# An attention and two mixtures of experts in one kernel: TensorE's work of a period regrouped by block size, and zero fills moved ahead of the weight stream

## The chip, the cores and the metric

One Trainium2 chip, one core. The time is that of the device in microseconds, the median of the runs of one program; lower is better. A second figure, the span, is taken from one profiled execution and runs from its first to its last instruction.

## The reference

Attention over 4 batches and 8 heads of 576 positions of 64 numbers: a band (each position sees those less than 4 away) plus a downsampled part (queries, keys and values averaged by 4, the result repeated 4 times). Its output, 2304 rows of 512, goes through a soft mixture (8 experts of 4 slots), and that result through a second mixture that routes each row to its best 2 of 8 experts. Everything is float32.

```python
q_d = q.reshape(B, H, Sd, factor, D).mean(axis=3)      # k_d, v_d alike, factor 4
out_up = np.repeat(sm_attn(q_d, k_d, v_d), factor, axis=2)
mask = np.abs(pos[:, None] - pos[None, :]) < factor
scores = np.where(mask, scale * q @ k.T, -1e9)
x = softmax(scores) @ v + out_up                       # then (B*S, H*D)
logits = x @ phi                                       # 2304 x 32 slots
slot_input = softmax(logits, axis=0).T @ x             # per expert 4 x 512
slot_out[e] = relu(slot_input[e] @ w1[e]) @ w2[e]
x = softmax(logits, axis=1) @ slot_out
noisy = x @ w_gate + log1p(exp(x @ w_noise)) * noise   # best two experts per row
out[rows of e] += weight * (relu(x @ w1[e]) @ w2[e])
```

## The kernel before

**Attention in 16 units.** A unit is one batch and two heads. The units are pipelined by hand: one period of the loop works on four of them, in the order of the string `SEQ` (L19), whose words are the steps in the table `BL` (L550). The words that matter here, with the line of their work: `S` the band's scores (mask L285, products L289) and `SD` the downsampled scores (L300), of unit p; of unit p-1 `CP` (L375) and `CD` (L386), which turn the band's and the downsampled weights, `VD` (L268, L272), which averages the values, `DP` (L414) and `DD` (L421), which multiply weights by values; of unit p-2 `EP` (L441, L443), which turns the finished rows back, and `LG` (L463, L465), the logits of the soft mixture; of unit p+1 `A0` and `A1` (L231), which turn keys and queries, and `ld` (L186), which loads them for p+2; `lV` (L207) loads values. Copies out of PSUM are `cp` (L219 on ScalarE, L221 on VectorE): `EP00` to `EP11` into `PT`, `ED0` and `ED1` into `PdT`, `X0` and `X1` into `xK`, `V0` and `V1` into `Vd`, `x0` and `x1` into `xT`; `XA` (L433) adds the downsampled part, `LA` (L472, L474) adds up the logits. Every engine runs its own steps in the order in which they are written; one engine waits for another by semaphores where data or a buffer asks for it. The four buffers named `t` (`tp`, L176) take turns for all that TensorE turns; `S`, `Sd` and `xl` have a bank or two of PSUM of their own. In three of the periods each of the steps `ST`, `SU`, `SU_`, `SE`, `SS` (softmax over rows, kept up from batch to batch, L479 to L528) and `SK` (L534) are added.

**The tail** (`TSEQ`, L21) ends the last three units and the slots' input. `R2` there puts the loads of weights 8 to 10 (`w8` to `w10`) on SyncE's queue.

**Soft mixture.** Eight experts; each has a first product `hp` (L795), a turn of the hidden values `ht` (`hidden_t`, L807), and a second product `yacc` (L817). The weights come by DMA in the order of use; SyncE issues all loads (L101), and from the fourth expert's on they wait for buffers that `hidden(0)` frees.

**Routing and second mixture.** Rows are scattered into a table `tab` in DRAM and gathered by expert; the products (L1054) hold most of the second half. `tab` and `out` have to be zero before: 27 pieces in the list `fills`, the first 7 of them `tab`'s (six of 256 KB, one of 64 KB), sent by `clear` (L109) from a tile of zeros after the last weights of the soft mixture.

**Blocks.** TensorE's array of 128 by 128 is used in blocks: 128 by 128, 128 by 64, 128 by 32, 64 by 64, 16 rows by 64. In the trace a row for TensorE names the block (`128*64`).

Of the kernel before, what the change touches and what calls it, by code (L numbers as in the profile page):

```python
# [17 lines left out]

SEQ = """S SK CP EP01 ld EP10 M EP00 ST SD CD z EP11 ED0 EL SS MD A0 ED1 EX a00 W a01 SU SU_ A1 P1 a100 a101  # L19
a110 a111 P0 KD DQ0 VD z DP V0 V1 DQ1 DX EP LG DD x1 LA lV x0 X1 SE RD DM X0 XA""".split()  # L20
TSEQ = """S:15 CP:14 W EP01:14 EP00:14 SD:15 M:15 EL:15 EP10:14 EX:15 EP11:14 CD:14 ED0:14 MD:15 SU:15 VD:14 DP:14 V0:14 V1:14 EP:13  # L21
# [11 lines left out]
NHOT = [4, 8]  # L33
N2 = 3


@with_exitstack
def attn_moe_moe_kernel(ctx: ExitStack, tc: tile.TileContext, q, k, v, moe_phi, moe_w1, moe_w2,
# [50 lines left out]

    phi4 = const.tile([128, 4, 4 * NS], F32, name="phi4")  # L90
    wgn = const.tile([128, 4, 2 * E], F32, name="wgn")
# [14 lines left out]
    LK = keep.tile([128, NTILE, NS], F32, name="LK")  # L106
    zero = keep.tile([128, 256], F32, name="zero")

    def clear():  # L109
        o = fills.pop(0)  # L110
        n = o.shape[0]
        return nc.sync.dma_start(out=o.rearrange("p (a c) -> p a c", a=2), in_=zero[0:n, None].to_broadcast([n, 2, 256]))


    with ExitStack() as tctx:
# [33 lines left out]
        PT = a2.tile([128, 5, 2, 128], F32, name="PT")  # L149
        P = a2.tile([128, NG, 64], F32, name="P")  # L150
        Vs = [(a1, a2)[i].tile([128, 5, 2, D], F32, name=f"V{i}") for i in range(2)]
        four = a2.tile([128, 9, 32], F32, name="four")
# [23 lines left out]
        def tp():  # L176
            return ps.tile([128, 512], F32, name="t", bufs=4)

        LD, VQ, KD, DQ, SD, SS, PD, PL, XL, XT, XK = ({} for _ in range(11))

# [80 lines left out]
        def v_pe(u):  # L261

            V = Vs[u % 2]
            XL[u] = ps.tile([128, 2, 512], F32, name="xl")
            t = XL[u][:, 0, 290:418]
            for d in range(2):
                for c in range(4):
                    nc.tensor.matmul(t[32 * c:32 * c + 32], four[:, 5 * d + c],  # L268
                                     V[:, c + d].rearrange("p h d -> p (h d)"), start=(d == 0), stop=(d == 1),
                                     skip_group_check=True)  # L270
            for h in range(2):
                nc.tensor.matmul(XL[u][0:32, h, 434:498], four[:, 4], V[:, 4, h], start=True, stop=True,  # L272
                                 skip_group_check=True)
            VQ[u] = (None, wk.tile([128, 2, 128], F32, name="Vd", bufs=1))

        def v_evac(u, i):
            xl, Vd = XL[u], VQ[u][1]
            if i:
                cp("v1", Vd[0:16, 1].rearrange("p (h d) -> p h d", h=2), xl[0:16, :, 434:498])
            else:  # L280
                cp("v0", Vd[:, 0], xl[:, 0, 290:418])

        def b_s(u):
            s = ps.tile([128, 512], F32, name="S")
            nc.tensor.matmul(s[:, 0:NG * KW], idb, mask.rearrange("p g k -> p (g k)"), start=True, stop=True)  # L285
            for g in range(NG):
                for a in range(2):
                    c0 = 58 * g + HQ * a
                    nc.tensor.matmul(s[64 * a:64 * a + 64, KW * g:KW * g + KW],  # L289
                                     Q[:, c0:c0 + 32].rearrange("p i h -> p (i h)"), K[:, c0:c0 + KW],  # L290
                                     start=False, stop=True, skip_group_check=True)
            SS[u] = s

# [86 lines left out]
        def c_d(u):  # L380
            Ed = PD.pop(u)
            tt = []
            for kb in range(2):
# [4 lines left out]
                tt.append(t)  # L388
            PdT = wk.tile([128, 2, 2, 144], F32, name="PdT", bufs=1)
            CT[u, 1] = (PdT, tt)  # L390

# [7 lines left out]
        def c_ed(u, kb):  # L399
            PdT, tt = CT[u, 1]  # L400
            n = (128, 16)[kb]
            cp(f"d{kb}", PdT[0:n, kb].rearrange("p h (a i) -> p h a i", a=3),
               tt[kb][0:n, 0:288].rearrange("p (a h i) -> p h a i", a=3, h=2))
# [13 lines left out]
        def d_d(u):  # L417
            xl, PdT, Vd = XL[u], CT[u, 1][0], VQ.pop(u)[1]
            for kb, n in enumerate((128, 16)):
                for h in range(2):  # L420
                    nc.tensor.matmul(xl[64 * h:64 * h + 64, 1, 290:434], Vd[0:n, kb, 64 * h:64 * h + 64], PdT[0:n, kb, h],  # L421
                                     start=(kb == 0), stop=(kb == 1), skip_group_check=True)
# [14 lines left out]
        def e_pe(u):  # L437
# [6 lines left out]
            ET_[u] = (t, t2)  # L444
            if u % 4 == 0:
                XK[u // 4] = xp.tile([128, 5, 4, 128], F32, name="xK", bufs=1)

        def e_evac(u, i):
            t = ET_[u][i]
            if i:  # L450
# [7 lines left out]

        def logit_pe(u, t2=None):
            xT, kk = XT[u], u % 4  # L460
            L = (ET_[u][1] if t2 is None else t2)[:, 128:320]
            for t in range(4):
                nc.tensor.matmul(L[32 * t:32 * t + 32, 0:128], phi4[:, kk, 0:NS], xT[:, 128 * t:128 * t + 128],  # L463
                                 start=True, stop=True, skip_group_check=True)
            nc.tensor.matmul(L[:, 128:192], phi4[:, kk], xT[:, 512:576], start=True, stop=True, skip_group_check=True)  # L465
            LL[u] = L

# [118 lines left out]
        for p in range(-1, NU - 1):  # L586
            if p == 0:
                nc.sync.dma_start(out=phi4[:, :, 0:NS], in_=moe_phi.rearrange("(k p) s -> p k s", p=128))
            if p >= 5 and small:
# [5 lines left out]
            for nm in SEQ:  # L595
# [8 lines left out]
                if p == -1 and nm == "lV":  # L604
                    nc.gpsimd.memset(PT, 0.0)
                if p == -1 and nm == "DQ1":
                    nc.vector.memset(P, 0.0)
            if p == 0:
                hot(NHOT[0])
                nc.vector.tensor_scalar(trib, jp, 0.0, None, op0=ALU.is_gt)  # L610
                consts()
            if p == 1:
                nc.vector.tensor_copy(phi4[:, :, NS:4 * NS].rearrange("p k (t s) -> p k t s", t=3),
                                      phi4[:, :, None, 0:NS].to_broadcast([128, 4, 3, NS]))
        m = ms_[(B - 1) % 2]
# [8 lines left out]
        def ring_2():  # L624
            actx.close()
            ring2 = rctx.enter_context(tc.tile_pool(name="ring2", bufs=1, reuse_waits="tile"))
            for i in range(NPRE, NPRE + N2):
                mload(i, ring2, (f"w{i}a", f"w{i}b"))
            flush()

        def max_t():
# [30 lines left out]
        def slot_in():  # L662
            t = tp()
            for kk in range(4):
# [5 lines left out]
              "SI": slot_in, "UA": lambda: slot_u(B - 1, (0, 1)), "UB": lambda: slot_u(B - 1, (2, 3)),  # L670
              "LG:15": lambda: logit_pe(NU - 1, tp()), "W": flush}
        TAIL.append(1)
# [42 lines left out]
    with ExitStack() as mctx:  # L715
# [85 lines left out]
        def hidden_t(e):  # L801
            hs_ = HS.pop(e)
            hz[e] = mw.tile([128, 2, 4, NS], F32, name="hz", bufs=3)
            nc.gpsimd.memset(hz[e], 0.0)
            ht_ = ps.tile([128, 2, 4, NS], F32, name="ht", bufs=1)
            for c in range(2):
                nc.tensor.transpose(ht_[:, c].rearrange("p j s -> p (j s)"), hs_[:, 128 * c:128 * c + 128], idf)  # L807
            nc.vector.tensor_scalar(hz[e][:, :, :, SPE * e:SPE * e + SPE], ht_[:, :, :, SPE * e:SPE * e + SPE],
                                    0.0, None, op0=ALU.max)

# [592 lines left out]
```

## Time and profile before

| | us |
|---|---|
| median of 3 runs | 496.57 (494.85 to 496.62) |
| the profiled execution's own time | 494.55 |
| its span | 492.7 |
| TensorE busy, matmuls | 470.2 (95% of the span) |
| VectorE, ScalarE, GpSimd busy | 277.4, 263.4, 199.2 |
| mean granted clock of TensorE | 0.987 |

How to read it: PE is TensorE, PEld its weight loads, DVE VectorE, ACT ScalarE, POOL GpSimd, SP SyncE, and SPq the queue of SyncE, where DMA issues show. L and a number is the line in the kernel. A bracket at a row's end tells how long the engine stood before it and for whom; "issue" is standing that nothing in the profile explains. Attention runs to about 150 us, its tail and the slots' input to 164 us, the soft mixture to about 200 us, the rest to 492.7 us.

### The profile page before, as it was taken

To read this page: it belongs to the slowest core of one execution; us is meant where nothing else is said; L and a number is where in the kernel's file an instruction comes from. 1 tells how busy PE (TensorE), PEld (TensorE's weight loads), DVE (VectorE), ACT (ScalarE), POOL (GpSimd) and SP (SyncE) were. 2 spreads that over 40 slices of the span, in tenths; PEclk is the share of its full clock that TensorE was granted. 3 is DMA by queue.
4 is the path that set the end of the run, shared out by engine and by line. 5 is a ranking of instruction groups with operands and counts; after the bars stand their busy time and mean duration, and the time that the engine had idled before them with its cause. 6 is when DMAs were issued, how large, how long until landed. Compare 5 with 4: busy or idle time off the path is not lost.

```text
span 492.7 us, 12033 instructions
## 1 busy us (share of the span) xinstructions
PE 470.2 (95%) x4569; PEld 355.9 (72%) x4569; DVE 277.4 (56%) x720; ACT 263.4 (53%) x698; POOL 199.2 (40%) x289
## 2 busy tenths in 40 slices
PE   5999999899998999899999999999999999999993
PEld 4688877777875543467787787887887887878882
DVE  7878877777875321696579545273462544624300
ACT  2567766666775021486365465483664746727410
POOL 5565636536540100166566677422222221222222
PEclk9999999999999799999999999999999999999997
DMA  9999998989979599999988744699958856333333
GB/s 160 278 243 214 233 221 192 242 216 202 265 239 345 171 393 399 389 346 338 365 258 228 224 75 76 150 363 297 275 72 229 216 128 154 43 45 43 45 43 46
DMA packets 108423, 104.16 MB, mean 211 GB/s; under 512 B 68170, under 2 KB 78090, under 8 KB 108362
## 3 DMA queue, kind: packets, MB, share of 16 engines
q1 hardware_dynamic: 101450, 90.50, 61.2%
q0 software_dynamic: 6912, 12.85, 16.6%
q8 instruction: 38, 0.62, 0.5%
q14 instruction: 23, 0.19, 0.1%
HBM read 83.60 MB, written 19.73 MB: 210 GB/s over the span
## 4 chain that ended last, share of the span: by engine, by line
PE 73%; issue 9%; DMA 7%; DVE 3%; POOL 2%; ACT 2%; POOLq 2%; SPq 0%; ACTq 0%; DVEq 0%
PE y L1054 34%; DMA wr<-in_moe_w_dram 5%; PE S L289 4%; PE t L231 3%; PE gx L871 3%; PE xl L421 3%; PE Sd L300 3%; PE xl L414 2%; PE t L375 2%; PE xl L268 2%; PE t L441 2%; PE h L1034 2%; PE t L386 2%; POOL out_dram L1073 2%; POOLq L1079 1%
## 5 line engine op out<-in xcount | busy, mean ns | idle before, releaser
L1054 PE MATMUL y<-whi,hl 128*128 128x512 f32 x320 | 127.3, 398 | 0.0
L1054 PE MATMUL y<-whi,hh 128*128 128x512 f32 x320 | 126.7, 396 | 0.4 <-ACT hh L1035 0.4
L1054 PE MATMUL y<-wlo,hh 128*128 128x512 f32 x320 | 126.5, 395 | 0.0
L1073 POOL DMA_INDIRECT out_dram<-ys,idx x40 | 64.5, 1612 | 107.9 <-ACT ys L1065 56.3
L1065 ACT ACTIVATE ys<-y,gt 128x512 f32<-128x512 f32 x40 | 27.4, 686 | 82.4 <-issue 46.9
L1026 DVE TENSOR_TENSOR wlo<-wr,whi 128x512 fp32r<-128x512 f32 x64 | 42.0, 692 | 50.3 <-ACT whi L1023 49.9
L1054 PEld LDWEIGHTS y<-wlo,hh 128*128 128x128 f32 x320 | 60.1, 188 | 12.9 <-issue 1.0
L1054 PEld LDWEIGHTS y<-whi,hl 128*128 128x128 f32 x320 | 60.1, 188 | 12.3 <-issue 2.1
L1054 PEld LDWEIGHTS y<-whi,hh 128*128 128x128 f32 x320 | 60.2, 188 | 11.8 <-ACT hh L1035 0.6
L333 POOL TENSOR_TENSOR P<-El,su 64x350 f32<-64x350 f32 x31 | 23.9, 772 | 59.7 <-DVE su L326 38.3
L1036 DVE SCALAR_TENSOR_TENSOR hl<-h,hh 128x256 fp32r<-128x256 f32 (+1 forms) x64 | 31.3, 489 | 16.0 <-ACT hh L1035 14.7
L1000 POOL DMA_INDIRECT tab<-stk,pos x36 | 35.6, 990 | 11.5 <-issue 10.7
L1036 DVE SCALAR_TENSOR_TENSOR hl<-gx,hh 128x256 fp32r<-128x256 f32 (+1 forms) x64 | 31.2, 487 | 10.7 <-ACT hh L1035 9.1
L1023 ACT ACTIVATE whi<-wr 128x512 fp32r<-128x512 f32 x64 | 36.9, 625 | 0.2
L1035 ACT ACTIVATE hh<-gx 128x256 fp32r<-128x256 f32 (+1 forms) x64 | 28.1, 439 | 15.0 <-PE gx L1034 12.5
L1035 ACT ACTIVATE hh<-h 128x256 fp32r<-128x256 f32 (+1 forms) x64 | 28.0, 437 | 12.5 <-PE h L1034 10.2
L1072 POOL MEMSET spacer<- 1x1 f32 x40 | 13.6, 340 | 41.6 <-issue 41.6
L219 ACT ACTIVATE PT<-t 64x256 f32<-64x256 f32 (+1 forms) x50 | 20.6, 417 | 13.5 <-PE t L375 12.7
L919 DVE TENSOR_TENSOR oh<-iot,R 128x256 fp32r<-128x256 f32 (+2 forms) x50 | 20.3, 439 | 11.4 <-PE xs L937 9.6
L231 PE MATMUL t<-idf,ld 96*128 96x96 f32 x192 | 21.1, 259 | 4.9 <-DMA ld<-in_k_dram 4.3
L219 ACT ACTIVATE xT<-xl 128x290 f32<-128x290 f32 x32 | 11.5, 411 | 26.2 <-PE xl L421 24.1
L289 PE MATMUL S<-K,Q 128*64 128x35 f32 x640 | 23.1, 231 | 2.2 <-issue 1.4
(301 smaller groups left out, 837.8 us busy)
## 6 DMA issues: line engine op xcount, KB each, us to landing
wr<-in_moe_w_dram SPq DMA_DIRECT2D x120, 256.0 KB, 5.6
wr<-in_moe_w_dram SPq DMA_DIRECT2D x56, 512.0 KB, 7.1
out_dram<-zero SPq DMA_DIRECT2D x20, 256.0 KB, 3.4
V<-in_v_dram SPq DMA_DIRECT2D x62, 80.0 KB, 5.2
ld<-in_k_dram SPq DMA_DIRECT2D x32, 144.0 KB, 4.7
ld<-in_q_dram SPq DMA_DIRECT2D x32, 144.0 KB, 4.4
XT<-tab SPq DMA_DIRECT2D x5, 320.0 KB, 5.6
tab<-zero SPq DMA_DIRECT2D x6, 256.0 KB, 4.8
```

The source lines that it names most:

```text
L219: nc.scalar.activation(dst, src, AF.Copy)
L231: nc.tensor.transpose(t[:, 96 * c:96 * c + 96], ld[:, i, 3 * j + c].rearrange("p h d -> p (h d)"), idf[0:96, 0:96])
L289: nc.tensor.matmul(s[64 * a:64 * a + 64, KW * g:KW * g + KW], Q[:, c0:c0 + 32].rearrange("p i h -> p (i h)"), K[:, c0:c0 + KW], start=Fals ...
L333: eng.tensor_tensor(P[as_, :, HQ * a:HQ * a + KW], El[as_], su[as_, :, None].to_broadcast([64, NG, KW]), op=ALU.mult)
L1000: st = nc.gpsimd.indirect_dma_start(out=tab, out_offset=bass.IndirectOffsetOnAxis(ap=pos[:, c, i:i + 1], axis=0), in_=stk[:, i].bitcast(F3 ...
L1023: nc.scalar.activation(whi[:, kk], wb(kk), AF.Copy)
L1026: eng.tensor_tensor(wlo[:, kk], wb(kk), whi[:, kk].bitcast(F32), op=ALU.subtract)
L1035: nc.scalar.activation(hh[:, f], h, AF.Relu)
L1036: nc.vector.scalar_tensor_tensor(hl[:, f], h, 0.0, hh[:, f].bitcast(F32), op0=ALU.max, op1=ALU.subtract)
L1054: nc.tensor.matmul(y, l[:, kk, ts_], r_[:, kk], start=(m == 0), stop=(m == 23))
L1065: nc.scalar.activation(ys, YS.pop((e, ti)), AF.Copy, scale=gt[:, ti:ti + 1])
L1073: st = nc.gpsimd.indirect_dma_start(out=out, out_offset=bass.IndirectOffsetOnAxis(ap=idx[:, ti:ti + 1], axis=0), in_=ys, in_offset=None, c ...
```

## The change

Seven edits.

1. In `SEQ`, `EP` stands behind `CP` (ahead of `SD`), `LG` behind `VD`, `DD` behind `DP`, ahead of the next period's mask; `X0` and `X1`, the copies of `EP`, stand behind `EP11`; `LA` behind `V1`; `SU_` behind `SD`.
2. The mask product is made in two blocks of 128 by 64 instead of one of 128 by 128.
3. The logits' last 64 columns are made in four products of 32 columns instead of one of 128, so `phi` is held once and not four times; the product goes to the bank of `S` in the loop.
4. `DD`'s second block has 128 rows, of which 112 are zeros set once, instead of 16 rows; `Vd` and `PdT` are fixed buffers.
5. `hidden_t` makes eight products of 32 columns that pick the expert's own 4 slots, instead of two full turns.
6. Seven zero pieces (`NZ`) are issued right behind the loads of `w8` to `w10`.
7. The tile of zeros is 512 wide, and a packet of it 2 KB instead of 1 KB.

```diff
-SEQ = """S SK CP EP01 ld EP10 M EP00 ST SD CD z EP11 ED0 EL SS MD A0 ED1 EX a00 W a01 SU SU_ A1 P1 a100 a101
-a110 a111 P0 KD DQ0 VD z DP V0 V1 DQ1 DX EP LG DD x1 LA lV x0 X1 SE RD DM X0 XA""".split()
+SEQ = """S SK CP EP01 ld EP10 M EP00 ST EP SD SU_ EP11 X0 X1 CD z ED0 EL SS MD A0 ED1 EX a00 W a01 SU A1 P1 a100 a101
+a110 a111 P0 KD DQ0 VD LG z DP V0 V1 LA DQ1 DX DD x0 x1 lV SE RD DM XA""".split()
...
+NZ = 7
...
-    zero = keep.tile([128, 256], F32, name="zero")
+    zero = keep.tile([128, 512], F32, name="zero")
...
-        return nc.sync.dma_start(out=o.rearrange("p (a c) -> p a c", a=2), in_=zero[0:n, None].to_broadcast([n, 2, 256]))
+        return nc.sync.dma_start(out=o, in_=zero[0:n])
...
-            nc.tensor.matmul(s[:, 0:NG * KW], idb, mask.rearrange("p g k -> p (g k)"), start=True, stop=True)
+            for a in range(2):
+                as_ = slice(64 * a, 64 * a + 64)
+                nc.tensor.matmul(s[as_, 0:NG * KW], idb[:, as_], mask.rearrange("p g k -> p (g k)"), start=True, stop=True,
+                                 skip_group_check=True)
...
-            for kb, n in enumerate((128, 16)):
+            for kb in range(2):
                 for h in range(2):
-                    nc.tensor.matmul(xl[64 * h:64 * h + 64, 1, 290:434], Vd[0:n, kb, 64 * h:64 * h + 64], PdT[0:n, kb, h],
+                    nc.tensor.matmul(xl[64 * h:64 * h + 64, 1, 290:434], Vd[:, kb, 64 * h:64 * h + 64], PdT[:, kb, h],
                                      start=(kb == 0), stop=(kb == 1), skip_group_check=True)
...
-            L = (ET_[u][1] if t2 is None else t2)[:, 128:320]
+            L = (tp() if TAIL else SB[u + 2])[:, 0:192]
...
-            nc.tensor.matmul(L[:, 128:192], phi4[:, kk], xT[:, 512:576], start=True, stop=True, skip_group_check=True)
+            for t in range(4):
+                nc.tensor.matmul(L[32 * t:32 * t + 32, 128:192], phi[:, kk], xT[:, 512:576], start=True, stop=True,
+                                 skip_group_check=True)
...
+                    nc.gpsimd.memset(Vd[:, 1], 0.0)
+                    nc.gpsimd.memset(PdT[:, 1], 0.0)
...
             flush()
+            for _ in range(NZ):
+                clear()
...
-                nc.tensor.transpose(ht_[:, c].rearrange("p j s -> p (j s)"), hs_[:, 128 * c:128 * c + 128], idf)
...
+                for j in range(4):
+                    nc.tensor.matmul(ht_[32 * j:32 * j + 32, c], hs_[:, 128 * c + 32 * j:128 * c + 32 * j + 32], own_,
+                                     start=True, stop=True, skip_group_check=True)
```

What it moves on TensorE in one period of the loop: first before (from `VD` to the next period's `CD`; lines 268 and 272 are `VD`, 414 `DP`, 421 `DD`, 285 and 289 mask and `S`), then after, where the same steps have lines 271 and 275, 418, 425, 289 and 294, and `EP` is 445 and 447, `LG` 467 and 470.

```order
L268 MATMUL xl<-V_133,four 32x128 x8
L272 MATMUL xl<-V_133,four 32x64 x2
L414 MATMUL xl<-PT,V_133 64x58 x20
L441 MATMUL t<-idf,xT 128x128 x4
L443 MATMUL t<-idf,xT 64x128
L463 MATMUL t<-xT,phi_79 32x128 x4
L465 MATMUL t<-xT,phi_79 128x64
L421 MATMUL xl<-PdT,Vd 64x144 x4
L285 LDWEIGHTS idb
L285 MATMUL S<-mask,idb 128x350
L289 MATMUL S<-K,Q 64x35 x20
L375 MATMUL t<-idf,P 128x128 x5
```

The same stretch of the period after:

```order
L271 MATMUL xl<-V_135,four 32x128 x8
L275 MATMUL xl<-V_135,four 32x64 x2
L467 MATMUL S<-xT,phi 32x128 x4
L470 MATMUL S<-xT,phi 32x64 x4
L418 MATMUL xl<-PT,V_135 64x58 x20
L425 MATMUL xl<-PdT,Vd 64x144 x4
L289 LDWEIGHTS idb
L289 MATMUL S<-mask,idb 64x350
...
L294 MATMUL S<-K,Q 64x35 x20
L380 MATMUL t<-idf,P 128x128 x5
```

Between `DP` and `DD` there stood `EP` and `LG`, ten products; now `DD` follows `DP` at once, and `LG` stands ahead of `DP`. The pair of rows of the mask comes twice (the second is left out).

On ScalarE in one period, before and then after, from the copies of `x0` and `x1` (`xT`) to those of the queries (`Q`); a period's row of `El` is the exponential of the band's scores.

```order
L219 ACTIVATE xT<-xl 128x5x58 x2
L219 ACTIVATE xK<-t 64x128
L219 ACTIVATE xK<-t 128x4x128
L219 ACTIVATE PT<-t 64x3x128
L219 ACTIVATE PT<-t 64x2x128 x2
L219 ACTIVATE PdT<-t 128x288
L219 ACTIVATE PdT<-t 16x288
L319 ACTIVATE El<-El 128x350
L219 ACTIVATE K<-t 128x288 x2
L219 ACTIVATE Q<-t 64x288 x2
```

ScalarE's period after:

```order
L222 ACTIVATE xT<-xl 128x5x58 x2
L222 ACTIVATE PT<-t 64x3x128
L222 ACTIVATE PT<-t 64x2x128 x2
L222 ACTIVATE xK<-t 128x4x128
L222 ACTIVATE xK<-t 64x128
L222 ACTIVATE PdT<-t 128x288
L222 ACTIVATE PdT<-t 16x288
L324 ACTIVATE El<-El 128x350
L222 ACTIVATE K<-t 128x288 x2
L222 ACTIVATE Q<-t 64x288 x2
```

The two copies into `xK` stood ahead of those into `PT`; now they stand behind them and ahead of `PdT`, `El`, `K` and `Q`.

On SyncE at the end of attention, before and then after: the loads of the weights 9 and 10, and what follows them.

```order
L101 DMA w9b<-in_moe_w_dram 128x512 x4
L101 DMA w10a<-in_moe_w_dram 128x1024 x2
L101 DMA w10b<-in_moe_w_dram 128x1024 x2
L101 DMA wr<-in_moe_w_dram 128x512 x8
L101 DMA wr<-in_moe_w_dram 128x1024 x4
```

SyncE's queue there after:

```order
L102 DMA w9b<-in_moe_w_dram 128x512 x4
L102 DMA w10a<-in_moe_w_dram 128x1024 x2
L102 DMA w10b<-in_moe_w_dram 128x1024 x2
L113 DMA tab<-zero 128x512 x6
L113 DMA tab<-zero 32x512
L102 DMA wr<-in_moe_w_dram 128x512 x8
L102 DMA wr<-in_moe_w_dram 128x1024 x4
```

The seven pieces of `tab` now stand between the last early weights and the stream `wr`; the 20 pieces of `out` stay where they were.

## Rows read from the trace of the kernel before

**Rows 1.** The page's part 4: the chain that ended last, by line.
```profile
PE y L1054 34%; DMA wr<-in_moe_w_dram 5%; PE S L289 4%; PE t L231 3%; PE gx L871 3%; PE xl L421 3%; PE Sd L300 3%; PE xl L414 2%; PE t L375 2%; PE xl L268 2%; PE t L441 2%; PE h L1034 2%; PE t L386 2%; POOL out_dram L1073 2%; POOLq L1079 1%
```
**Rows 2.** Windows, one period: stretch, its length, busy us by engine, clock, DMA share, GB/s.
```profile
114.28:122.68 8.40, 8.40 (x155) 6.84 (x154) 6.51 (x18) 5.92 (x20) 4.83 (x8) 1.00 1.08 231
```
**Rows 3.** Timeline of that period's start: start us, us, engine line, operation, idle before.
```profile
111.34 0.81 PE L414 MATMUL xl<-PT,V 64*64 64x58 f32 x40
111.51 0.83 DVE L221 COPY Q<-t 64x288 f32<-64x288 f32 x2
112.38 0.48 DVE L221 COPY Vd<-xl 128x128 f32<-128x128 f32 x2
112.77 0.16 PEld L463 LDWEIGHTS t<-xT,phi 128*32 128x32 f32 x8 [0.20 <-issue]
113.13 0.30 PEld L465 LDWEIGHTS t<-xT,phi 128*128 128x128 f32 x2 [0.20 <-issue]
113.89 0.19 PEld L421 LDWEIGHTS xl<-PdT,Vd 16*64 16x64 f32 x4 [0.20 <-issue]
114.28 0.10 PEld L285 LDWEIGHTS <-idb 128*128 128x128 bf16 x1 [0.20 <-issue]
114.54 1.25 PEld L289 LDWEIGHTS S<-K,Q 128*64 128x64 f32 x40 [0.16 <-issue]
```
**Rows 4.** Chain of waits, same period and the next: start us, us, what.
```profile
112.15 0.59 PE t L441 x4
...
112.85 0.36 PE t L463 x8
...
115.90 0.70 PE t L375 x5
```
**Rows 5.** Chain of waits in the tail, unit 15's products.
```profile
150.75 0.78 PE xl L414 x40
...
151.56 0.49 DVE Vd L221 x2
...
152.18 0.88 PE xl L421 x8
```
**Rows 6.** Timeline, ScalarE in the periods around 108 to 115 us.
```profile
108.08 1.29 ACT L219 ACTIVATE PT<-t 64x384 f32<-64x384 f32 x3 [1.16 <-PE t L375]
...
109.39 0.69 ACT L219 ACTIVATE PdT<-t 128x288 f32<-128x288 f32 x2
...
115.00 0.75 ACT L219 ACTIVATE xK<-t 64x128 f32<-64x128 f32 x2
```
**Rows 7.** Timeline, VectorE in a period with slots.
```profile
63.99 0.64 DVE L528 COPY U<-t 128x512 f32<-128x512 f32 x1
```
**Rows 8.** Timeline, SyncE's queue: unit 15's queries are issued (two loads).
```profile
127.85 2.02 SPq L186 DMA_DIRECT2D ld<-in_q_dram  x2
```
**Rows 9.** The page's part 6: loads of queries, KB each, median us to landing.
```profile
ld<-in_q_dram SPq DMA_DIRECT2D x32, 144.0 KB, 4.4
```
**Rows 10.** Timeline, TensorE turns unit 15's queries.
```profile
136.91 0.71 PE L231 MATMUL t<-idf,ld 96*128 96x96 f32 x6
```
**Rows 11.** Timeline, SyncE's queue around the start of the soft mixture.
```profile
155.91 0.87 SPq L101 DMA_DIRECT2D w10b<-in_moe_w_dram  x2
166.36 8.75 SPq L101 DMA_DIRECT2D wr<-in_moe_w_dram  x14
```
**Rows 12.** Windows of the same stretch, columns as in rows 2.
```profile
160.00:162.00 2.00, 2.00 (x17) 1.13 (x9) 0.86 (x3) 0.00 (x0) 0.84 (x16) 0.50 0.91 371
...
164.00:166.00 2.00, 2.00 (x18) 0.97 (x21) 0.49 (x2) 0.00 (x0) 0.00 (x0) 0.50 0.00 0
```
**Rows 13.** Line 112, issues of the zero pieces: ns min/median/max, first and last start.
```profile
L112 SPq DMA_DIRECT2D tab<-zero x7: 620/638/1500, 203.3 to 208.0; - x7
```
**Rows 14.** Groups by line, 160 to 200 us: busy us, mean ns, idle before.
```profile
L807 PE MATMUL ht<-idf,hs 128*128 128x128 f32 x16 | 3.5, 300 | 0.0
```
**Rows 15.** Chain of waits after the first experts.
```profile
170.05 5.40 DMA wr<-in_moe_w_dram
```

## What the change should do to the time

> **What bounds the kernel now.** I read the chain that ended last first, then the attention stretch, where six of the seven edits lie, and last the soft mixture. The chain [rows 1] gives its largest share to the second mixture's products (L1054, 34%), which the change does not touch; the steps that it moves or remakes (L289, L231, L421, L300, L414, L441) have 2 to 4% each. In a steady period of the loop [rows 2] TensorE is busy 8.40 of 8.40 us at a granted clock of 1.00, and DMA too has a share of about 1 (1.08). So a period ends when TensorE ends, but the loads are close behind: unit 15's queries are issued in two loads that take 2.02 us of SyncE's queue from 127.85 [rows 8], the second at about 128.9, and one lands 4.4 us later [rows 9], at about 133.3; TensorE turns them at 136.91 [rows 10]. That is a lead of 3.6 us, after which loads and not TensorE would pace the loop. In the tail the chain runs DP, copy of Vd, DD [rows 5]: there TensorE does wait.
>
> **Attention, what goes.** In one period the weight loads stand five times for "issue", always where the block changes: 0.20 ahead of L463, 0.20 ahead of L465, 0.20 ahead of the 16-row half of L421, 0.20 ahead of the mask, 0.16 ahead of the scores, 0.96 together [rows 3]. After the change LG follows VD at 32 columns, the logits' last product has 32 columns too, both halves of DD and the mask and the scores are all 128 by 64: these five gaps go. Against that stand three more small products and a second weight load of the mask, which I size at 0.14: L463's eight rows take 0.36 with a gap of 0.20 in it [rows 4], so 0.02 each, and the second half of the mask counts for most of the rest. If nothing waits, a period is 0.82 shorter. The Trainium skill, "TensorEngine Tiling (Array Packing)", Key Properties, states that changing the tiling mode drains the engine; the 0.20 us gaps agree.
>
> **Attention, what comes.** The old order had EP and LG between DP and DD; the chain prices L441 at 0.59 and L463 at 0.36 [rows 4]; with L443 as a quarter more of L441 and L465 like L463 that is about 1.4 us. Vd's copy ran under them: in the period shown it starts at 112.38, after DP's last product at 112.15, and takes 0.48 [rows 3, 4]. It does not start earlier after the change, since the copy waits for the whole of DP (both are in the tile xl), and DD needs it. With DD right behind DP nothing covers it. The tail shows that order already: DP ends at 151.53, the copy starts at 151.56 and takes 0.49, DD starts at 152.18 [rows 5]; TensorE stands 0.65. By this row I charge 0.70 per period (0.65, and in the loop VectorE's Q copies, 0.83, may still be ahead of Vd [rows 3]). Bounds: 0 if the copy somehow got ahead, 1.0 if Q's copies delay it by as much as half of one. What is queued behind the waiting DD on TensorE is the mask and the scores of the next unit; ScalarE's copies of x wait for DD, and so does everything that follows from it.
>
> On ScalarE the copies into xK (0.75) now stand ahead of those into PdT (0.69), El, K and Q [rows 6]. TensorE's CP takes 0.70 [rows 4], EP by L441 and its fifth turn 0.7 too, and SD, in three wide products, I take to be as long, so CD could start 2.1 us after CP; the copies of PT, 1.29 us [rows 6], starting about 0.64 into CP, free its buffer at 1.9 to 2.0: just in time. Then xK until 2.75 and PdT until 3.45 hold back the turn of queries, which could start at 3.2: 0.2 to 0.3. The loss is passed on to Q's copies and by them to DP in part; I take 0.07 per period, the difference from working the period through step by step (8.34 against 8.394). Bounds 0 and 0.5.
>
> So a period comes out at −0.82 + 0.70 + 0.07 = −0.05. Thirteen such periods: −0.7. The first two of the loop have no EP or LG to lose as cover and gain about 0.2 each by the cheaper mask and DD: −0.4. In the three periods with slots VectorE's update of U (0.64 [rows 7]) now stands ahead of El, and xK's copies wait for one more step on TensorE; half of the 0.64 is hidden by the wait for scores, so +0.35 each: +1.0. The loop together: −0.1, between −3 and +3.
>
> The Trainium skill's same page, PSUM Bottleneck, says that tiling speeds up TensorE but not the evacuation of PSUM, which then becomes the bound; it is the rule against this change. The stand of 0.65 at the tail's DP and DD agrees with it.
>
> **The tail** keeps its order and has the waits already. There the gaps go for nothing in return: DD(14) and DD(15) 0.20 and about 0.05 of shorter products each, three logits with 0.20 each on the chain, of which one is beside a wait: about −0.9 (−0.5 to −1.3).
>
> **The soft mixture.** L807 takes 3.5 us in 16 matmuls [rows 14], 0.37 per expert on the chain; eight products of 16 columns take about 0.25 less with the block changes gone. Over eight experts that would be 2 us, but the chain passes to the weights from 170.05 on, with 5.40 us in its first step [rows 15]: the stream starts at 166.36 [rows 11], when the first expert's product frees the buffers, and it runs at its own pace. Only what lies behind the last weights counts: −0.3 (0 to −0.8).
>
> **The zeros.** Seven pieces take 0.62 to 0.64 us of SyncE each (one of the seven 1.50), at 203.3 to 208.0 now [rows 13]. They move to just behind w10b, whose issue ends at 156.8 [rows 11]; they are then issued by 161.5, before SyncE needs the stream at 166.36. Their bytes, 1.64 MB, at the 371 GB/s that the end of the early weights moves in 160 to 162 take 4.4 us; in 164 to 166 DMA stands still (0.00) [rows 12]. They follow the early weights from about 162 and end near 166.5, so about when the stream begins. Cost 0, bounds −0.3 and +1.5. What they free, 6 us of queue from 203.3 on, lies where the chain is TensorE's L1054 and no row of the chain is DMA: 0. The wider packets: no row shows either form to be faster where it would count, 0.
>
> **Sum.** −0.1 − 0.9 − 0.3 + 0 = −1.3 us, so 494.55 → 493.25 in the profiled execution's terms. That execution is 2.0 us below the median of the three runs (496.57), which alone spread over 1.8; on the median, 495.3. Less than 0.5% (2.5 us) is what a measurement of this kernel can tell from no change.
>
> **Rivals.**
> A. The copy of Vd gets hidden after all (it runs once VD has written its values, with DP still at work, or TensorE's stand falls together with a wait that is there anyway), so the period gains 0.82. Against: rows 5. For: the gaps are real. It would be 0.82 in some thirteen periods, 10.7 us, but the lead of 3.6 us in the loads is used up and the loop then follows the DMA share near 1: about −3. With tail and mixture −4.2: 492.3.
> B. The same without that cap, if loads, whose queue waits for no TensorE step, run ahead as TensorE does: −10.7 − 1.2, so about 485. Against: the DMA share of 1.08 in the period.
> C. Slower: evacuation takes over as the bound. xK's 0.75 ahead of PdT, El, K and Q makes Q's copies late, so that Vd starts late and DP, DD and x follow; ScalarE is busy 5.92 and VectorE 6.51 of 8.40 [rows 2], so there is room in sum but not in sequence. It decides from the point where the copies lie 0.3 us per period behind the 0.77 I charge: 13 × 0.3 = +3.9 on the loop's −0.1, and −1.2 from the rest: 499.2.
> D. The zeros delay the first weights by 1 to 2 us, and the soft mixture with them: +1.5 on the sum, 496.8. For: they end within a us of the stream's start. Against: DMA has these 4.4 us to spare.
>
> By the tiling page's rule of draining alone, all gaps saved would give rival B's time; the rule of evacuation gives my forecast or C.
>
> **Chances.** The forecast and D together .54 (D .08 of it), A .22, B .08, C .16. Faster by over 0.5% (below 494.1): A and B, and the forecast's lower end, .06: .36. Slower by over 0.5% (above 499.05): half and more of C plus the forecast's upper end: .16. The same: .48. Range: the forecast's own is 493 to 498; it is drawn out to take in A and most of C: 490.8 to 499.8, which leaves out B and the worse end of C.
>
> **What would show it.** In the new trace: per period the five gaps gone from the weight loads; a wait of L425 (DD) on the copy of Vd (L224) of about 0.7 us in every period; periods of about 8.3. If no such wait is there and periods are about 7.6 to 8.1, A or B is right, and then TensorE waits for loads at L234 (A) or not (B). A wait of L418 (DP) or L234 on ScalarE's copies of over 0.3 per period would be C. The tab pieces at about 157 to 161.5 on SyncE's queue, with the stream's first weights no later against hidden(0) than now; if they are, D. The turn of the hidden values (L816) shorter by 0.25 per expert, with the chain still passing over weights near 170. The forecast is wrong if the loop's length from the first to the last score differs by more than 3 us from before.

## The result and the profile after

| | before | after |
|---|---|---|
| median of 20 runs each, us | 495.99 (491.89 to 500.45) | 499.05 (496.21 to 504.17) |
| ratio, 95% interval | 1 | 1.0075 (1.0053 to 1.0097) |
| the profiled execution's own time, its span | 494.55, 492.7 | 500.02, 498.2 |
| TensorE busy | 470.2 | 463.1 |

The kernel became slower by 0.75%, some 3.7 us. TensorE has 7 us less to do and ends later. The profiled execution of after is 1 us above its median, that of before 1.4 below, so their difference, 5.5, overstates the loss by about 2 us. Of these 5.5 us, 1.7 lie before DP of unit 15 (3.1 without a stand of 1.4 us in before's loop, see below), 2.5 between it and the first product `hp` of the soft mixture (13.7 us in before, 16.2 in after), 0.1 in the soft mixture, and 1.2 behind it, a stretch that scatters more widely than that among all the profiles (293.8 to 297.0 us).

Windows of after, columns as in [rows 2]: a normal period, then one with slots, each from the mask's first product to the next.

```profile
122.55:130.79 8.24, 7.59 (x164) 6.88 (x160) 6.56 (x18) 5.92 (x20) 4.82 (x8) 1.00 1.01 243
130.79:143.01 12.22, 10.04 (x182) 7.40 (x178) 8.97 (x24) 7.39 (x27) 4.86 (x8) 1.00 0.79 213
```

The normal period fell from 8.40 [rows 2] to 8.24, with TensorE now busy 7.59: 0.65 of standing took the place of most of the 0.81 saved. The timeline shows where [rows 3, 4]:

```profile
120.55 0.81 PE L418 MATMUL xl<-PT,V 64*64 64x58 f32 x40
...
121.48 0.48 DVE L224 COPY Vd<-xl 128x128 f32<-128x128 f32 x2 [0.23 <-PE xl L418]
...
122.01 0.71 PE L425 MATMUL xl<-PdT,Vd 128*64 128x144 f32 x8 [0.65 <-DVE Vd L224]
...
122.55 0.32 PE L289 MATMUL S<-mask,idb 128*64 128x350 bf16 x2
```

DD follows DP's end by the copy of Vd and no longer has an `issue` gap between its halves, nor has the mask behind it. The waits of TensorE in the loop (30 to 140 us of after): what waits, for whom, us in total, times, longest.

```profile
PE xl L425 <- DVE Vd L224: 7.7, 12, 0.7
PE t L391 <- ACT xK L222: 1.0, 2, 0.7
PE t L447 <- ACT Et L516: 0.9, 2, 0.4
PE t L512 <- ACT ET L492: 0.8, 2, 0.4
PE t L391 <- DMA V<-in_v_dram: 0.4, 1, 0.4
PE t L445 <- DVE xT L437: 0.3, 1, 0.3
PE xl L418 <- issue: 0.3, 1, 0.3
```

All but the first row and the last lie in the three slot periods. From the first product of DP of one unit to that of the next, read off the trace of each kernel, us:

| period to unit | before | after | order alone | blocks alone | old order in slot periods | old order |
|---|---|---|---|---|---|---|
| 3 (normal) | 8.40 | 8.25 | 8.90 | 8.01 | 8.24 | 8.05 |
| 5 (slots) | 10.02 | 10.93 | 11.56 | 9.62 | 9.09 | 9.66 |
| 9 (slots) | 11.71 | 11.95 | 11.90 | 10.27 | 9.91 | 10.02 |
| 13 (slots) | 10.20 | 12.22 | 11.89 | 10.16 | 9.91 | 9.80 |
| DP of unit 15 starts at | 150.68 | 152.41 | 159.19 | 147.17 | 147.94 | 146.86 |

Before's 11.71 holds a stand of 1.4 us within the scores that no other profile has at that place. So the slot periods cost 0.91, 1.64 (from 10.31) and 2.02 more, 4.6 in all; against a second profile with the old order and blocks (the run with the zeros alone, below: 10.50, 10.20, 10.44) it is 4.0. One of them in after, timeline:

```profile
131.62 0.94 POOL L252 TENSOR_TENSOR s<-Q 64x288 f32<-64x288 f32 x1
131.66 0.92 DVE L487 TENSOR_TENSOR ms<-ms,ms 128x1 f32<-128x1 f32 x1
...
132.80 0.40 ACT L492 ACTIVATE ET<-LT,nm 128x128 f32<-128x128 f32 x1 [1.07 <-DVE nm L489]
...
133.35 0.33 PE L512 MATMUL t<-idf,ET 128*128 128x128 f32 x1 [0.40 <-ACT ET L492]
...
135.10 0.30 PE L447 MATMUL t<-idf,xT 128*64 128x128 f32 x1 [0.44 <-ACT Et L516]
...
137.89 0.75 ACT L222 ACTIVATE xK<-t 128x512 f32<-128x512 f32 x2 [2.44 <-PE t L391]
...
138.54 0.41 PE L391 MATMUL t<-idf,Ed 96*16 96x96 f32 x3 [0.66 <-ACT xK L222]
```

and the same steps before:

```profile
131.24 0.16 DVE L481 TENSOR_TENSOR ms<-ms,ms 128x1 f32<-128x1 f32 x1
131.27 0.94 POOL L249 TENSOR_TENSOR s<-Q 64x288 f32<-64x288 f32 x1
...
131.95 0.40 ACT L486 ACTIVATE ET<-LT,nm 128x128 f32<-128x128 f32 x1
...
133.22 0.27 PE L506 MATMUL t<-idf,ET 128*128 128x128 f32 x1
```

Before, the first exponentials were done 0.9 us ahead of their turn (132.35, 133.22); after, ST, EP's last turn and CD each stand at the head of TensorE's queue for something that ScalarE makes in a row, and the products of `SU_` (1.34 us) now lie ahead of CD.

The tail after: its logits stand once for nothing that the profile shows, and the zero pieces, issued from 203.3 us on before [rows 13], now take SyncE's queue from 158.24 to 166.06 (forecast: done by 161.5). The windows are to be read against [rows 12].

```profile
157.38 0.30 PE L467 MATMUL t<-xT,phi 128*32 128x128 f32 x1 [0.74 <-issue]
```
```profile
158.24 7.82 SPq L113 DMA_DIRECT2D tab<-zero  x7
```
```profile
162.00:166.00 4.00, 4.00 (x26) 2.37 (x22) 1.68 (x6) 0.00 (x0) 1.32 (x18) 0.50 0.97 328
166.00:170.00 4.00, 3.32 (x23) 1.79 (x27) 0.78 (x3) 0.00 (x0) 0.72 (x5) 0.50 0.70 266
```

### The profile page after: what moved, and what is told of

Same layout as the page of the kernel before. It is cut to its first block, busy times and chain, and to the rows that moved or that the text cites. A ratio compares the mean times of both kernels' runs of the same rounds, so it can differ in the third digit from the quotient of the medians.

```text
span 498.2 us, 12459 instructions
## 1 busy us (share of the span) xinstructions
PE 463.1 (93%) x4793; PEld 358.2 (72%) x4793; DVE 278.6 (56%) x719; ACT 264.0 (53%) x698; POOL 199.4 (40%) x291
## 4 chain that ended last, share of the span: by engine, by line
PE 47%; issue 4%; DVE 2%; POOLq 1%; ACT 1%; POOL 1%; DVEq 0%
PE y L1063 39%; PE gx L880 3%; PE h L1043 2%; PE gx L1043 2%; PE xs L946 1%; POOLq L1088 1%; DVE hl L1045 1%; POOL out_dram L1082 1%; PE xs L1024 1%; PE xs L943 0%; DVE wlo L1035 0%; ACT ys L1074 0%; ACT hh L1044 0%; PE gx L960 0%; ACT whi L1032 0%
## 5 line engine op out<-in xcount | busy, mean ns | idle before, releaser
L1045 DVE SCALAR_TENSOR_TENSOR hl<-h,hh 128x256 fp32r<-128x256 f32 (+1 forms) x64 | 31.4, 490 | 16.0 <-ACT hh L1044 13.7
L294 PEld LDWEIGHTS S<-K,Q 128*64 128x64 f32 x640 | 22.3, 143 | 1.2 <-issue 1.0
L896 DVE TENSOR_TENSOR GS<-gx,ghi 32x256 fp32r<-32x256 f32 x28 | 11.8, 420 | 19.8 <-ACT ghi L890 19.3
```

Source lines behind the costliest of these rows:

```text
L1045: nc.vector.scalar_tensor_tensor(hl[:, f], h, 0.0, hh[:, f].bitcast(F32), op0=ALU.max, op1=ALU.subtract)
```

## The experiments

Ratios are to the kernel before on the same chip. Three chips were used, and the changed kernel itself ran again only on the last of them, that of the two runs with the old order and of its own second run, where its ratio was 1.0155. Elsewhere a comparison with its 1.0075 is one between sessions.

**Blocks and order apart.** The old order with the new mask, logits and DD:

```diff
-            nc.tensor.matmul(s[:, 0:NG * KW], idb, mask.rearrange("p g k -> p (g k)"), start=True, stop=True)
+            for a in range(2):
+                as_ = slice(64 * a, 64 * a + 64)
+                nc.tensor.matmul(s[as_, 0:NG * KW], idb[:, as_], mask.rearrange("p g k -> p (g k)"), start=True, stop=True,
...
-            for kb, n in enumerate((128, 16)):
+            for kb in range(2):
```

> The kernel before with the new blocks alone: the mask in two halves, four small last products of the logits, DD's second block with 128 rows; the order of the steps, the zeros and the hidden values as before. Theory (the gaps at block changes are real costs and EP and LG still cover the copy of Vd, so the new order is what gave the gain away): of the five gaps of a period four go, periods of 7.8 to 8.0 us instead of 8.39 until the loads catch up, 3 to 7 us less than before, ratio 0.986 to 0.994. Rival (gaps come back elsewhere, or the period is set by something behind TensorE): periods of 8.3, ratio 0.997 to 1.000.

Measured 0.9939 (0.9900 to 0.9978): faster. Timeline of it, then its waits in the loop:

```profile
46.61 0.66 PE L444 MATMUL t<-idf,xT 128*128 128x128 f32 x4
46.93 0.48 DVE L223 COPY Vd<-xl 128x128 f32<-128x128 f32 x2
47.10 0.27 PE L446 MATMUL t<-idf,xT 128*64 128x128 f32 x1
47.30 0.16 PEld L466 LDWEIGHTS t<-xT,phi 128*32 128x32 f32 x8 [0.20 <-issue]
```
```profile
PE t L390 <- ACT Et L515: 1.2, 2, 0.6
PE S L293 <- issue: 1.2, 1, 1.2
PE t L233 <- DMA ld<-in_q_dram: 0.8, 2, 0.6
```

The copy of Vd runs under EP, one gap of five is left, and in the second half TensorE waits for loads of queries: the lead of the loads is used up. The four gaps are worth more than the period shows: from the first product of DP to that of CP it is 0.66 shorter (3.83 us for 4.49), and 0.22 of that is lost again at SD, whose weights now wait for Dq from GpSimd:

```profile
34.51 0.73 PEld L304 LDWEIGHTS Sd<-kd,Dq 128*96 128x96 f32 x6 [0.28 <-POOL Dq L253]
```

The reverse, the new order on the kernel before:

```diff
-SEQ = """S SK CP EP01 ld EP10 M EP00 ST SD CD z EP11 ED0 EL SS MD A0 ED1 EX a00 W a01 SU SU_ A1 P1 a100 a101
+SEQ = """S SK CP EP01 ld EP10 M EP00 ST EP SD SU_ EP11 X0 X1 CD z ED0 EL SS MD A0 ED1 EX a00 W a01 SU A1 P1 a100 a101
...
```

> The kernel before with the new order of the steps alone (and the logits in the scores' bank, which that order needs); blocks, zeros and hidden values as before. Theory (the order is what costs: Vd uncovered by 0.65 us per period, EP at the head of TensorE's queue in the slot periods; the new blocks gave 2 to 4 us back): periods of 8.6 to 8.9 us instead of 8.39, slot periods of 11 to 13 instead of 10.0 to 10.3, slower by 5 to 10 us, ratio 1.010 to 1.020. Rival (order and blocks are both near zero, and tail, zeros or hidden values make the loss): within 2 us, ratio 0.998 to 1.004.

Measured 1.0197 (1.0150 to 1.0245): the order is the loss. Its waits:

```profile
PE xl L421 <- DVE Vd L221: 7.8, 12, 0.7
PE t L443 <- ACT Et L510: 0.9, 2, 0.5
PE t L386 <- ACT xK L219: 0.8, 2, 0.4
```

**The uncovered copy.** VD's product in spare columns of the scores' bank, so that the copy waits for VD and not for DP:

```diff
-            t = XL[u][:, 0, 290:418]
+            VS[u] = sv = SB[min(u + 1, NU - 1)]
+            t = sv[:, 192:320]
```

> The changed kernel with the averaged values (VD) in spare columns of the scores' bank instead of the bank that DP writes, so that the copies V0 and V1 can run beside DP. Theory (DD stands 0.64 us in each of 12 periods for Vd only because the copy waits for DP, and nothing else is close behind): the wait of DD for Vd goes, periods fall from 8.25 to 7.6 to 7.8 us until the loads catch up, 4 to 7 us less than the changed kernel, ratio 0.993 to 0.999. Rival A (loads of keys and queries cap the loop): TensorE waits at the turn of keys for DMA, at most 3 us less, ratio 1.002. Rival B (ScalarE's copies of PT, xK, PdT are as late): DP or CD waits for ScalarE by about as much, under 1 us less.

Measured 0.9976 (0.9943 to 1.0010), 1% below the changed kernel. The wait only halved, since Q's copies on VectorE come next in the copy's way (timeline below), and the period is 8.00, with a wait of SD for Dq as in the run of the blocks alone:

```profile
PE xl L426 <- DVE Vd L224: 3.5, 12, 0.4
```
```profile
119.34 0.84 DVE L224 COPY Q<-t 64x288 f32<-64x288 f32 x2
120.21 0.48 DVE L224 COPY Vd<-S 128x128 f32<-128x128 f32 x2
```

LG between DP and DD instead of ahead of DP:

```diff
-a110 a111 P0 KD DQ0 VD LG z DP V0 V1 LA DQ1 DX DD x0 x1 lV SE RD DM XA""".split()
+a110 a111 P0 KD DQ0 VD z DP V0 V1 LG LA DQ1 DX DD x0 x1 lV SE RD DM XA""".split()
```

> The changed kernel with the logits (LG) between DP and DD instead of ahead of DP. Theory (0.65 us of standing at DD is covered by about 0.6 us of LG, at the price of one more change of block): the wait of DD for Vd falls from 0.64 to below 0.2 us, the period from 8.25 to 7.8 to 8.0 us, 2 to 5 us less than the changed kernel, ratio 0.997 to 1.003. Rival (Q's copies on VectorE hold Vd as long): the wait stays above 0.4, ratio 1.006.

Measured 1.0053 (1.0023 to 1.0083), periods of 8.05, unclear against the changed kernel; the wait is 3.6 us in 11 times here, 0.33 each, between theory and rival.

**The slot periods.** Three attempts to mend a single step. The second buffer (this kernel leaves a part of the slots' sums out, so only its times are read):

```diff
-                XK[u // 4] = xp.tile([128, 5, 4, 128], F32, name="xK", bufs=1)
+                XK[u // 4] = (xp.tile([128, 5, 128], F32, name="xA", bufs=2), xp.tile([128, 5, 3, 128], F32, name="xK", bufs=1))
```

> The changed kernel with a second buffer for the first unit of a batch in xK, so that its copies on ScalarE need not wait for the slots' products of the batch before (four more small products per slot period). Theory (in three periods X0 waits 2.2 to 2.4 us for SU_ at the head of ScalarE's queue, with PdT, El, K and Q behind it): these waits go, the slot periods fall from 10.93, 11.95 and 12.22 us to about 10.2, 11.2 and 11.0, 2 to 3 us less in all, ratio about 1.002. Rival (the slot periods are long because TensorE itself does SU_ ahead of CD, or because the exponentials of the slots come late): less than 0.7 us in all, ratio 1.006.

1.0064 (1.0032 to 1.0095); slot periods 10.67, 11.67 and 11.95: 0.27 each, 0.8 in all, far nearer to the rival. CD no longer waits for xK; EP's last turn still waits 0.4 us. The exponentials earlier:

```diff
-a110 a111 P0 KD DQ0 VD LG z DP V0 V1 LA DQ1 DX DD x0 x1 lV SE RD DM XA""".split()
+a110 a111 P0 KD DQ0 VD LG z DP V0 V1 LA SE DQ1 DX DD x0 x1 lV RD DM XA""".split()
```

> The changed kernel with the slots' exponentials (SE) right behind the addition of the logits instead of behind the copies of x. Theory (in the three slot periods ST stands at the head of TensorE's queue, with EP, SD, SU_ and CD behind it, until the exponentials are there, which come 2.0 us after the mask's product where they came 0.9 us after it before; the reduce of Dq and a VectorE instruction of 0.92 instead of 0.16 us lie ahead of them): the waits of ST, EP's last turn and CD fall by 0.7 to 1.2 us in each slot period, 2 to 3 us in all, ratio about 1.002. Rival (the slot periods are long because SU_ is in the way of CD and X0): under 0.7 us in all, ratio 1.006 to 1.0075.

1.0123 (1.0084 to 1.0162), slot periods 11.71, 12.10 and 12.10: both theory and rival fell. ST waits no more, but x's copies now come behind the exponentials, and EP waits for xT (first row below; from the window of one slot period). The turn of the exponentials later, and xT's addition ahead of them:

```diff
-SEQ = """S SK CP EP01 ld EP10 M EP00 ST EP SD SU_ EP11 X0 X1 CD z ED0 EL SS MD A0 ED1 EX a00 W a01 SU A1 P1 a100 a101
+SEQ = """S SK CP EP01 ld EP10 M EP00 EP SD EP11 ST SU_ X0 X1 CD z ED0 EL SS MD A0 ED1 EX a00 W a01 SU A1 P1 a100 a101
...
```

> The changed kernel with xT's addition (XA) ahead of the slots' exponentials on VectorE, and the turn of the exponentials (ST) behind EP and SD on TensorE and its copies behind EP11 on ScalarE. Theory (in a slot period x's copies, its addition and the exponentials stand in a row on ScalarE and VectorE, and since EP moved to the period's front whichever of EP and ST comes second waits for the whole row): no wait of EP and ST in the slot periods, 0.7 to 1.5 us less in each, ratio 1.001 to 1.004. Rival (it is the products SU_ ahead of CD and the copies X0 behind them that set the length): under 0.5 us per slot period, the wait stays with CD; ratio 1.006.

1.0199 (1.0151 to 1.0246), slot periods 11.87, 12.36, 12.63: worse again, ST now waits for PT's copies to free a turning bank (second fence).

```profile
PE t L445 <- DVE xT L437: 1.6, 1, 1.6
```
```profile
PE t L512 <- ACT PT L222: 1.4, 1, 1.4
```

Then the old order (SEQ0, the string of before) in these three periods alone:

```diff
-            for nm in SEQ:
+            for nm in SEQ0 if r4 == 1 and b4 >= 0 else SEQ:
```

> The changed kernel with the old order of the steps in the three slot periods alone; the new order in all others. Theory (the part of the loss that the forecast missed lies in these three periods, and it is the new order that makes them long: 10.93, 11.95 and 12.22 us against 10.0 to 10.3 before): they fall to 9.8 to 10.4 us, 4 to 5 us less than the changed kernel, ratio 0.997 to 1.000. Rival (what is saved there comes back in the next period, where EP, turned to the front, follows at once, or in the tail and the soft mixture): less than 2 us, ratio 1.004 to 1.0075.

1.0000 (0.9966 to 1.0035), 0.75% below the changed kernel's first ratio and 1.5% below that on this chip; slot periods 9.09, 9.91 and 9.91, the periods behind them 0.65 longer (9.30 and 9.33 for 8.65 and 8.68), DP of unit 15 at 147.94 instead of 152.41. Of the waits of ST, EP and CD in the slot periods only those of ST are left (second row), and DD's wait is gone there too (first row, 10 times instead of 12):

```profile
PE xl L427 <- DVE Vd L226: 6.4, 10, 0.7
PE t L514 <- ACT ET L494: 0.8, 2, 0.4
```

The whole loop in the old order, all else as changed:

> The changed kernel with the old order of the steps in the whole loop; blocks, logits' bank, zeros and hidden values as changed. Theory (the order alone makes the loss; zeros, packets and the tail's banks are worth nothing beside it): as the blocks with hidden_t, ratio 0.990 to 0.996. Rival (the zeros ahead of the stream and the tail's banks make up to 1.5 us of the loss): ratio 0.996 to 1.000.

0.9976 (0.9940 to 1.0011): in the rival's range, with an interval that reaches well into the theory's, and 1.8% below the changed kernel on this chip.

**Zeros, banks, hidden values.** The zeros put back:

> The changed kernel with its seven early zero pieces put back behind the last weights of the soft mixture; all else as changed. Theory (the zeros cost nothing, the soft mixture's start is set by TensorE): ratio to before about 1.007, as the changed kernel's 1.0075, and the first product of the soft mixture starts no earlier than 168.0 us. Rival (the zeros hold DMA until 168 us and delay the end of attention or the first weights): 1.5 to 3 us less, ratio about 1.002, DMA still in 164 to 168 us and hp starting about 167 us.

1.0056 (1.0020 to 1.0093), not to be told from 1.0075. The first product of the soft mixture started at 166.1 us, earlier than the theory allowed, but in this profile the clock stayed at 1.00 there, so it does not decide. The same with VD's bank:

> The changed kernel with VD in the scores' bank (as in the run of that alone, ratio 0.9976) and the seven zero pieces back behind the weights. Theory (from 150 to 198 us DMA is the limit whenever TensorE keeps its full clock, so 1.64 MB of zeros ahead of the stream push its last weights back by up to 4 us, less where DMA stood still): 2 to 4 us less than with VD's bank alone, ratio 0.990 to 0.994, the second products of the soft mixture end 3 us sooner after the start of the first. Rival (the zeros fit in a pause of DMA, as forecast): the same ratio, 0.998.

0.9957 (0.9924 to 0.9991) against 0.9976: not told apart either. In the profiles the second products do end 3.1 us sooner after the first `hp` (33.3 us for 36.4), as the theory has it, but with VD's bank alone the clock was 0.50 from 188.8 to 195.7 us. The zeros alone, on the kernel before:

> The kernel before with one edit: the first seven zero pieces (1 KB packets) issued right behind the early weights. Theory (the zeros delay the stream of weights where the clock stays full): slower by 1 to 3 us, ratio 1.002 to 1.006. Rival (forecast: they fit in a pause of DMA): ratio 1.000, within 0.5 us. Rival 2 (the earlier zeros free the queue at 203 us): 0.998.

1.0004 (0.9974 to 1.0034). What the ratios cannot tell shows in the five profiles in which the clock stayed at 1.00 from DP of unit 15 to the end of the last second product. That stretch takes 46.5 us in this run and 46.4 in the one with the old order in the slot periods, both with early zeros, and 45.0, 44.5 and 44.7 in three with late zeros (zeros put back, the same with VD's bank, blocks with hidden_t). So early zeros seem to hold the end of the soft mixture back by 1.4 to 2.0 us; the kernels differ in more than the zeros, so this is not a test of them alone. The tail's logits back in their old bank:

> The changed kernel with the tail's logits of units 13 and 14 in the spare columns of the bank of their turned rows, as before, so that two fewer of the four turning banks are used up and hp falls on the bank it had before. Theory (hp waits 0.68 us for the copy of the last logits because the turns of the banks have shifted, and this gap keeps the granted clock at 0.50 until 173 us instead of 166 us): no wait of hp for LK, clock back at 1.00 by 169 us, 2 to 3.5 us less than the changed kernel, ratio about 1.002. Rival (the low clock has to do with the standing at 156 to 158 us alone): the 0.68 us go, the clock stays at 0.50 until about 172 us, ratio 1.006.

1.0079 (1.0039 to 1.0119): the wait of hp for LK (0.7 us in after) is gone, the time is not less. In its profile the low clock did not come in 158 to 170 us at all, but neither did it in the run with late zeros, which has that wait; so the theory fell. hidden_t with the blocks, on the old order:

> The kernel before with the new blocks (0.9939 alone) and the new hidden_t; order and zeros as before. Theory (the soft mixture is paced by its weights, so hidden_t is worth nothing): ratio 0.992 to 0.996, as the blocks alone. Rival (a shorter turn per expert counts, 0.25 us each): 1 to 2 us less, ratio 0.990 to 0.992. In both cases faster than before and after.

0.9925 (0.9888 to 0.9962), not to be told from 0.9939: hidden_t is worth nothing that these runs can tell. This version beats both kernels.

**The changed kernel again.**

> The changed kernel again, on the same chip as the two others: its ratio to before here, and which of its waits come back in a second profile. Theory (the waits of the slot periods and of DD are fixed by the order; the stall inside the tail's logits and the place of the low clock are not): slot periods of 10.9, 11.9 and 12.2 us and 12 waits of DD of 0.64 us again, ratio 1.005 to 1.010; the low clock in another place or of another length. Rival: all of it repeats to 0.1 us.

1.0155 (1.0093 to 1.0216) on this chip, more than expected; the interval only just meets that of the first measurement. Slot periods 10.93, 11.92 and 12.21 and the 12 waits of DD came again (first row), with a stand of 3.2 us in one DD (second row). Against the expectation, the stand of 0.74 in the tail's logits came again too, at the same place, and so did the low clock behind it: 13.7 us of it, from about 6.9 us after the start of DP of unit 15 on, in both profiles (third row, windows; in after from 159.3 to 172.9). The first `hp` starts 16.2 us after that DP in both.

```profile
PE xl L425 <- DVE Vd L224: 7.7, 12, 0.7
PE xl L425 <- issue: 3.2, 1, 3.2
```
```profile
166.93:180.58 13.65, 12.79 (x88) 6.75 (x91) 4.01 (x18) 1.75 (x9) 2.03 (x21) 0.50 0.77 271
```

## Why the prediction was wrong

- **The direction.** −1.3 us was forecast, and the kernel is 3.7 us slower. The loop's part was put at −0.1; DP of unit 15 comes 1.7 us later in the profiles, 3.1 without before's stand of 1.4. The prediction's own sign, the loop's length from the first to the last score off by more than 3 us, was not met only because of that stand (134.47 and 136.26 us, +1.8).
- **Normal periods: right.** Forecast 8.34, by gaps of 0.82 less and a wait of 0.70 more; measured 8.25, the wait 0.64 in 12 periods. That the wait eats the gain is shown from both sides: blocks alone give periods of 8.00, the order alone 8.90, with 7.8 us of waits (7.7 in after), and moving VD's bank halves the wait. Of the nine normal periods eight are 0.08 to 0.15 shorter, where 0.05 was forecast, and one, with a stand, is 0.4 longer. The rule on evacuation that the prediction weighed stands in the Trainium skill ("TensorEngine Tiling (Array Packing)", PSUM Bottleneck) with a "may", and for a speedup of 4x. The trace agrees, and without such a speedup: 0.64 of 0.82 us went to one copy.
- **Slot periods: the step that failed.** "half of the 0.64 is hidden by the wait for scores, so +0.35 each: +1.0" measured 0.91, 1.64 and 2.02, together 4.6. The step priced VectorE's update of U and one wait of xK. It left out that EP, moved to the front of TensorE's period next to ST, and CD behind it need results that ScalarE and VectorE make one after the other (copies of x, exponentials, their copies), with copies of PT in the same queue. That the order of the steps in these periods is the cause is shown: the old order there alone took 4.5 us off at unit 15, brought the ratio to 1.000, and left no wait of EP or CD. It spares DD's wait in these periods as well, which is up to 2 of the 4.5. That the row of results is what makes the order costly is read from the waits. The three edits that each took one wait away do not contradict it: one gained 0.27 a period, the two others got a longer wait in its place.
- **First two periods: wrong by a little.** −0.4 forecast; 21.84 for 22.01 and 8.38 for 8.01, so +0.2.
- **The tail: wrong in the sum.** The last two units gained 0.95 (periods 6.61 and 4.79 for 7.19 and 5.16), as forecast. Behind them after lost 2.5 us up to the first `hp`, a term that the prediction does not have: the stand of 0.74, the 0.7 us that hp waits for LK, and above all a low clock to 173 us instead of 166. Both profiles of the changed kernel have all three. Where the clock stayed at 1.00 in the same tail, `hp` came 11.2 to 13.0 us after DP of unit 15 (seven profiles), not 16.2. The 13.0 is the run with LG between DP and DD, which has the stand and the wait for LK; so these account for some 1.8 us, and some 3.1 are left for the clock. The mean granted clock of the 20 runs is 0.986, that of the runs of before in a later session 0.988: what part of the loss hangs on the clock, and why it fell, stays open.
- **Soft mixture and zeros: no cost that the ratios can tell.** hidden_t shows in neither ratio; its products take 2.4 us in all for 3.5, 0.14 per expert and not 0.25. The zeros ended near 168 us and not at 166.5: DMA had no pause in which to take them, its share is 0.88 or more from 153 to 168 us in after. Rival D is not refuted: the five profiles at full clock speak for 1.4 to 2.0 us, and the old order with zeros, packets and banks as changed (0.9976) stands 0.5% above the blocks with hidden_t (0.9925), on another chip and with intervals that overlap.
- **Rival C** gave 499.2 and the median is 499.05, which is luck. Its place was wrong: ScalarE's copies are not late in every period (0.3 over the charge), only where the slots' steps are added to them.

## What to carry to other kernels

A change of the array's block showed here as a gap of 0.16 to 0.20 us, and four of them less, with the products added for it, as 0.66 us of a period. Grouping by block pays only where the work moved away covered nothing: what stood between a product and the one that needs its copied-out result was the cover, so price the copy's wait before moving it. Where a loop has odd periods, work the new order through each kind of period separately, from every engine's queue; three odd ones decided this result. Keep the two edits apart when they can be: the blocks without the order were the gain.

## What the runs showed that was not expected

A VectorE instruction on 128 by 1 numbers took 0.92 us instead of 0.16 where it started 0.04 us behind a GpSimd addition of 0.94 us (the two timelines of the slot period); the exponentials that needed it started 2.0 us behind the mask's first product instead of 0.9. The same instruction (`ms<-ms,ms`) shows it in other profiles too: it took 0.65 us where it started 0.31 behind the addition (the order alone), 0.28 where it started 0.68 behind it (blocks with hidden_t), and each time it ended 0.02 us after the addition. The Trainium skill, "GPSIMD Engine Reference", Specifications, says that GpSimd shares its SBUF interface with VectorE and that the two contend where a VectorE instruction has two SBUF inputs, as this one has; the 0.92 us agree.

Most profiles also have stands of TensorE "for issue" in the midst of a run of like products, of 0.2 to 3.2 us: 30 of them from 20 us on, in 15 of the 17 profiles. A long one moves a run by more than the changes of all normal periods add up to. Most stand at a place of their own, but the 0.74 us in the tail's logits came in four profiles, each time 5.0 us after the start of DP of unit 15. The traces point to what they hang on. The DMA queue `q8`, of the kind that the page calls instruction, carries packets of 16 KB (below, from the page of after: packets, MB, share of 16 engines). Every one of the 30 stands ends 1.25 to 1.69 us after such a packet has landed, although up to 205 us the packets come only about every 8 us. That TensorE stood for its next instructions is the reading that fits; no run tested it.

```profile
q8 instruction: 40, 0.66, 0.5%
```
